# A planned state-space and feed-forward kernel: a new order of work, and dummy products in TensorE's planned pauses

## The chip, the cores and the metric

The kernel runs on one core of a Trainium2 chip. The metric is the device time of one execution in microseconds (us). A core has TensorE for matrix products (PE in the profile, its weight loads PEld), VectorE (DVE), ScalarE (ACT), GpSimd (POOL) and SyncE (SP), which issues the DMAs here. Each engine carries out its own list of instructions strictly in order; the engines wait for one another through semaphores.

## The reference

There are 4 batches, 8 heads, 768 positions, head size 32 and state size 16. A linear recurrence runs along the positions and its result goes through a feed-forward layer with 2048 hidden units. The recurrence is written by chunks:

```python
cum = np.cumsum(log(a) of the chunk)
L = np.exp(cum[i] - cum[j]) * (i >= j)
y_intra = ((Cc @ Bc.T) * L) @ xc
y_inter = (Cc @ state) * exp(cum)
state = exp(cum[-1]) * state + (Bc * exp(cum[-1] - cum)).T @ xc
# all y of the heads side by side: x of 3072 x 256
h = x @ w_in
out = (h - np.tanh(h)) @ w_out
```

## The kernel before, in words

**The recurrence.** Positions are cut into 28 chunks of up to 112 (7 for each batch); the 16 state rows are put in front of a chunk's 112 rows as if they were positions, so that a chunk is one product over 128 rows. The first three chunks (`first_tile`) get their decay matrix from sums on TensorE (`cp`) and exponentials on ScalarE with a bias `ncum`. The other 25 (`chunk_a`) get it from a product of two bf16 tables `lt_c` and `rt_c` (9 rows deep, PE L455) that are put together from the running sums: VectorE splits the sums in three bf16 parts (`split`), SyncE writes them to memory (`cum`, L767) and reads them back into the tables (L773 and L775, eight DMAs for the first 7 chunks and eight for the rest). Ahead of these DMAs, `lt_c` is filled with ones (ACT L712), and `rt_c` with the ones times a sign that alternates over the partitions (DVE L433, two operations for each of the two spans). For every chunk then follow the exponential (ACT L465), the multiplication with the `att` product (DVE L469), the causal mask (POOL L472), and `chunk_y`: the product `y` (PE L497), the new state copied into the next chunk's operand (ACT L510), and `y` split in a high and a low part (ACT L517, DVE L522). One `att` tile and one `y` tile exist, so chunk follows chunk.

**The feed-forward layer.** 12 tiles of 256 positions; 8 steps for each tile. A step is `mm1` (12 products into `ph`, L548), tanh, a subtraction, a split in high and low (`act`), and `mm2` (12 products into `o`, L598). The first four tiles are gone through in four sweeps of two steps, with partial sums kept in `pt` (`keep`), the others in one go; `store` adds up and sends the result out. Weights arrive as 64-bit floats (`raw`, 1 MB for each of the 8 steps) and are turned into a high and a low part `wh`, `wl` by `conv` (two operations on ACT, five on DVE).

**What sets the order.** All operations are recorded with an engine, a cost and their inputs and outputs in `Order`; a list scheduler (`schedule`) places them by priority against a model with one queue for each engine, `plan` improves the priorities by 16 rounds and 1500 random changes, and `issue` emits the instructions in the order of the planned starts. The costs are numbers in the calls `op(engine, cost, ...)`. Pools of tiles fix how many of each tile live at once: two `ph`, one `o`, one `att`, one `y`.

## Time and profile before

| | |
|---|---|
| median of 3 runs | 341.84 us (340.10 to 342.27) |
| profiled execution | 341.82 us |
| its span | 340.1 us |
| PE busy | 325.4 us (96%) |
| DVE, ACT, POOL busy | 227.0, 193.0, 58.1 us |
| PE busy in the first 60 us (six windows of 10) | 7.96, 6.78, 6.54, 9.97, 7.64, 10.00 us |
| mean granted TensorE clock | 0.968 of full speed |

The span runs from the first to the last instruction; the execution's time is 1.7 us longer. Busy time is the time in which at least one instruction of the engine runs. The granted clock is a share of TensorE's full speed. In a row of the trace, the first number is the start and the second the length in us, and square brackets hold the idle time of the engine before it with what ended it. In the table of windows, a row holds the stretch, its length, then busy us and the number of instructions of PE, PEld, DVE, ACT and POOL, the granted clock, the DMA share and GB/s.

### The profile page before, as it was taken

What the parts mean: (1) busy time and instruction counts of PE and PEld (TensorE: products, weight loads), DVE (VectorE), ACT (ScalarE), POOL (GpSimd) and SP (SyncE); (2) the same over time, 40 slices, a digit from 0 to 9 for tenths busy, and PEclk for the clock granted to TensorE, in tenths of its full rate; (3) what the DMA queues carried; (4) which work ended last, traced back from release to release, by engine and by line L of the source; (5) the groups of instructions that cost most, each with busy time, mean ns of one, the idle gap of its engine ahead of it and who ended that gap; (6) DMA issues with size and microseconds to landing.
All of it is one profiled execution on the core that took longest, in us unless ns stands there. A gap on an engine that the chain in (4) does not pass through costs nothing.

```text
span 340.1 us, 8905 instructions
## 1 busy us (share of the span) xinstructions
PE 325.4 (96%) x3772; PEld 313.0 (92%) x3772; DVE 227.0 (67%) x339; ACT 193.0 (57%) x403; POOL 58.1 (17%) x69
## 2 busy tenths in 40 slices
PE   7839979999999999999999999999999999999995
PEld 6738879999999999999999999999999999999995
DVE  4996797999899875645655555654745554654552
ACT  7855977787564453544655555545555545544451
POOL 1544354350000110100311210210301110110000
PEclk9955989999999999999999999999999999999999
DMA  7929657714000011101110200300200000000100
GB/s 161 308 59 322 171 144 196 225 44 143 1 2 3 0 62 46 48 2 46 60 47 19 76 2 2 91 2 9 87 2 1 33 2 2 33 0 2 33 0 32
DMA packets 12471, 21.39 MB, mean 63 GB/s; under 512 B 2848, under 2 KB 7648, under 8 KB 12432
## 3 DMA queue, kind: packets, MB, share of 16 engines
q1 hardware_dynamic: 12432, 20.84, 21.6%
q8 instruction: 29, 0.48, 0.6%
q14 instruction: 10, 0.08, 0.1%
HBM read 17.51 MB, written 3.32 MB: 61 GB/s over the span
## 4 chain that ended last, share of the span: by engine, by line
PE 85%; DVE 6%; DMA 4%; SPq 2%; issue 1%; ACT 1%
PE o L598 40%; PE ph L548 38%; PE y L497 3%; DMA raw<-w_d 3%; PE att L461 3%; DMA bc<-bc_d 1%; PE att L455 1%; SPq L773 1%; DVE lt L407 1%; DVE wm L313 1%; PE y L505 1%; DVE wv L310 1%; DVE wm L305 1%; DVE wl L324 1%; SPq L775 0%
## 5 line engine op out<-in xcount | busy, mean ns | idle before, releaser
L562 ACT ACTIVATE g<-ph 128x512 f32<-128x512 f32 x96 | 57.4, 598 | 87.2 <-PE ph L548 86.5
L566 DVE TENSOR_TENSOR g<-ph,g 128x512 f32<-128x512 f32 x96 | 65.9, 689 | 59.7 <-ACT g L562 59.7
L548 PE MATMUL ph<-xh,wh 128*128 128x256 f32 x384 | 100.4, 285 | 0.0
L548 PE MATMUL ph<-xh,wl 128*128 128x256 f32 x384 | 99.1, 282 | 0.0
L577 DVE TENSOR_TENSOR gl<-g,gh 128x512 fp32r<-128x512 f32 x96 | 66.9, 700 | 26.9 <-ACT gh L570 25.7
L548 PE MATMUL ph<-xl,wh 128*128 128x256 f32 x384 | 76.4, 281 | 0.0
L570 ACT CAST gh<-g 128x512 fp32r<-128x512 f32 x96 | 59.1, 618 | 28.8 <-DVE g L566 27.3
L548 PEld LDWEIGHTS ph<-xh,wh 128*128 128x128 f32 x384 | 73.9, 192 | 1.0 <-issue 0.4
L548 PEld LDWEIGHTS ph<-xh,wl 128*128 128x128 f32 x384 | 74.1, 193 | 0.0
L472 POOL TENSOR_SCALAR_AFFINE_SELECT lt<-lt 128x896 f32<-128x896 f32 (+1 forms) x25 | 34.0, 1360 | 202.1 <-DVE lt L469 202.1
L598 PE MATMUL o<-gh,wh 128*128 128x256 f32 x384 | 63.0, 286 | 0.0
L548 PEld LDWEIGHTS ph<-xl,wh 128*128 128x128 f32 x384 | 59.5, 193 | 0.0
L598 PE MATMUL o<-gh,wl 128*128 128x256 f32 x384 | 59.4, 277 | 0.0
L598 PE MATMUL o<-gl,wh 128*128 128x256 f32 x384 | 59.3, 277 | 0.0
L598 PEld LDWEIGHTS o<-gh,wh 128*128 128x128 f32 x384 | 50.9, 188 | 2.7 <-issue 0.2
L598 PEld LDWEIGHTS o<-gh,wl 128*128 128x128 f32 x384 | 51.0, 188 | 0.0
L598 PEld LDWEIGHTS o<-gl,wh 128*128 128x128 f32 x384 | 50.8, 188 | 0.0
L469 DVE TENSOR_TENSOR lt<-att,lt 128x896 f32<-128x896 f32 (+1 forms) x25 | 26.7, 1067 | 7.2 <-ACT lt L465 7.2
L465 ACT ACTIVATE lt<-att 128x896 f32<-128x896 f32 (+1 forms) x25 | 22.6, 903 | 6.5 <-PE att L461 4.7
L510 ACT COPY x<-y 16x64 f32<-16x64 f32 x96 | 19.6, 204 | 8.9 <-DVE xl L522 7.5
L497 PE MATMUL y<-lt,x 128*32 128x112 f32 (+1 forms) x448 | 17.4, 276 | 5.5 <-POOL bc L355 2.9
L497 PEld LDWEIGHTS y<-lt,x 128*32 128x32 f32 x448 | 10.4, 113 | 9.2 <-POOL bc L355 3.1
(70 smaller groups left out, 232.4 us busy)
## 6 DMA issues: line engine op xcount, KB each, us to landing
raw<-w_d SPq DMA_DIRECT2D x16, 512.0 KB
x<-x_d SPq DMA_DIRECT2D x14, 256.0 KB
bc<-bc_d SPq DMA_DIRECT2D x56, 60.0 KB
out_d<-ob SPq DMA_DIRECT2D x24, 128.0 KB
braw<-bn_d SPq DMA_DIRECT2D x14, 112.0 KB
cum<-parts SPq DMA_DIRECT2D x1, 168.0 KB
rt_c<-cum SPq DMA_DIRECT2D x4, 27.0 KB
lt_c<-cum SPq DMA_DIRECT2D x4, 27.0 KB
```

What stands on the lines that cost most here:

```text
L461: nc.tensor.matmul(out=at_[:, i, 2 + w, :], lhsT=bb[r, w], rhs=cc[r, w, 0:q], start=True, stop=True)
L465: nc.scalar.activation(k["l"][:, :, 0:q].rearrange("p (i w) q -> p i w q", i=4), k["a"][:, :, 0:2, :], AF.Exp)
L469: nc.vector.tensor_tensor(out=lt, in0=k["a"][:, :, 2:4, :], in1=lt, op=ALU.mult)
L472: nc.gpsimd.affine_select(out=k["l"][:, :, 0:q], in_=k["l"][:, :, 0:q], pattern=[[0, H], [1, q]], compare_op=ALU.is_ge, fill=0.0, base=N, ...
L497: nc.tensor.matmul(out=y[D * h : D * h + D, hg * Q : hg * Q + q], lhsT=d["x"][:, cg, P * hg + D * h : P * hg + D * h + D], rhs=k["l"][:, 4 ...
L510: nc.scalar.copy(grp[(ck + 1) // CPG]["x"][0:N, (ck + 1) % CPG, 2 * D * i : 2 * D * i + 2 * D], k["y"][D * i : D * i + N, H * D : H * D + ...
L548: nc.tensor.matmul(out=ph[:, j, :], lhsT=w_[:, u, 0, k, j * P : (j + 1) * P], rhs=d[("xh", "xl")[p]][:, k, ts], start=p == 0 and k == 0 an ...
L562: nc.scalar.activation(g, gs[t, u][0], AF.Tanh)
L566: nc.vector.tensor_tensor(out=g, in0=ph, in1=g, op=ALU.subtract)
L570: nc.scalar.copy(gh, gs[t, u][1])
L577: on.tensor_tensor(out=gl, in0=g, in1=gh.bitcast(F32), op=ALU.subtract)
L598: nc.tensor.matmul(out=po[t, seg][:, e, :], lhsT=w_[:, u, 1, j, e * P : (e + 1) * P], rhs=g[:, j, :], start=u == seg[0] and k == 0 and j = ...
```

## The change

- The search for the order: other costs for many operations, six starts of the random climb in place of one (seeds 5 to 10 in place of one seed), and a rule that the parts of one load are issued in turn.
- Dummy products: where the plan has a pause on TensorE of over 0.35 us in the first 65 us of planned time, `issue` now calls `fill`, which puts (pause - 0.35) / 0.215 products of ones with ones behind the operation, of the same form as those of `warm`. They write to a part of the tile `pq2` (one PSUM tile of the pool that `o` uses) that nobody reads. They start once `pq2` exists and end with the first `mm2`, which takes that tile's place.
- Work moves between engines: the filling of `lt_c` with ones from ACT to POOL; the identity rows of the three `braw` tiles (`stay`) from DVE to POOL; the sign product of `rt_c` for the second span (two operations of 2304 columns) from DVE to POOL, while that of the first span stays on DVE; the copy of the sums (`rows`) and their negation (`ncum`) from DVE to ACT.
- The partial sums `pt` and the outgoing tiles `ob` (four and two buffers) become one ring of six, which `rows` and `rest` use before; the first four tiles are added up in place.

The diff, cut to its core (further costs change as the two in the first lines of `conv` do):

```diff
+LULL, SPARE, PIECE = 65.0, 0.35, 0.215
+NPT = 6
-    ROUNDS, JITTER, SEED, CLIMB, RAMP = 16, 0.3, 133908, 1500, 110.0
+    ROUNDS, JITTER, SEED, CLIMB, RAMP, STARTS = 16, 0.3, 5, 1500, 110.0, 6
...
                 if dma and self.ops[j][0] == "DMA":
                     chain.add(j)
+                    soft.add(j - 1)
                     hard |= self.before[n]
...
     def plan(self):
+        _, span, start, _ = min((self.climb(random.Random(self.SEED + k)) for k in range(self.STARTS)), key=lambda b: b[0])
+        return span, start
...
         _, start = self.plan()
-        for i in sorted(range(n), key=lambda i: (start[i], i)):
+        order = sorted(range(n), key=lambda i: (start[i], i))
+        pe = [i for i in order if self.ops[i][0] == "PE"]
+        lull = {i: start[j] - start[i] - self.ops[i][1] for i, j in zip(pe, pe[1:])}
+        for i in order:
             if self.ops[i][2]:
                 self.ops[i][2]()
+            if start[i] < LULL and lull.get(i, 0.0) > SPARE:
+                self.fill(int((lull[i] - SPARE) / PIECE))
...
-            op("ACT", 1.0 * k, lambda s=s: fn0(s), r=n_r, w=[n_v[i]])
+            op("ACT", 1.17 * k, lambda s=s: fn0(s), r=n_r, w=[n_v[i]])
...
+    def fill(pieces):
+        one = nc.const_aps.tensor(1.0, (P, P), F32)
+        for _ in range(pieces if "pq2" in misc else 0):
+            nc.tensor.matmul(out=misc["pq2"][0:32, 3 * P :], lhsT=one[:, 0:32], rhs=one, start=True, stop=True)
...
-                    op("DVE", (0.3, 0.8)[s], lambda w=w, sl=sl: nc.vector.tensor_scalar(
+                    eng, on = (("DVE", nc.vector), ("POOL", nc.gpsimd))[s]
+                    op(eng, (0.45, 2.5)[s], lambda w=w, sl=sl, on=on: on.tensor_scalar(
                            out=rt_c[:, w, sl], in0=lt_c[:, sl], scalar1=par[:, w : w + 1], scalar2=None, op0=ALU.mult),
...
+            misc.pop("pq2", None)
             if u == seg[0]:
                 po[t, seg] = ps_o.tile([P, 2, TT], F32, tag="po", name=f"o{t}_{u}")
...
-        n_pt[t] = slot("pt", NSW)
+        n_pt[t] = slot("pt", NPT)
...
-        name = op.pieces(slot("ob", 2), 2)
+        name = [n_pt[t]] * 2 if t < NSW else op.pieces(slot("pt", NPT), 2)
...
         for t in braws:
-            nc.vector.tensor_copy(out=t[0:N].rearrange("p c (h n) -> p (c h) n", h=H),
+            nc.gpsimd.tensor_copy(out=t[0:N].rearrange("p c (h n) -> p (c h) n", h=H),
...
-        nc.scalar.copy(v, nc.const_aps.tensor(1.0, (P, 1), F32).broadcast_to(v.shape))
+        nc.gpsimd.memset(v, 1.0)
...
-            nc.vector.tensor_copy(out=rows[r], in_=misc["pr"][r, 0:2])
+            nc.scalar.copy(rows[r], misc["pr"][r, 0:2])
...
+    def negate():
+        nc.scalar.activation(ncum.rearrange("p h c -> p (h c)"), misc["pq"][:, 0:NHC], AF.Copy, scale=-1.0)
...
+    op.fill = fill
     op.issue()
```

How the change stands in the lists of the engines. TensorE before, around the second and third `y` of the first tile, down to the first product of the tables (a number behind a name tells buffers apart; `y` is the chunk's product, `att` of `rt_c` the first decay product, `ph` an `mm1`):

```order
L384 MATMUL cp_1_304<-upto,la 128x112 x4
L497 MATMUL y_323<-lt_239,x_151 32x112 x8
L505 MATMUL y_323<-x_151,bw_250 16x32 x8
L497 MATMUL y_369<-lt_289,x_159 32x112 x8
L505 MATMUL y_369<-x_159,bw_269 16x32 x8
L455 LDWEIGHTS lt_c
L455 MATMUL att_392<-rt_c,lt_c 128x224
```

The same place now; `pq` is the tile that takes the dummy products:

```order
L400 MATMUL cp_1_298<-upto,la 128x112 x4
L389 MATMUL pq_202<-const-float32-1.0 32x128 x4
L514 MATMUL y_329<-lt_228,x_146 32x112 x8
L522 MATMUL y_329<-x_146,bw_259 16x32 x8
L389 MATMUL pq_202<-const-float32-1.0 32x128 x13
L514 MATMUL y_384<-lt_272,x_233 32x112 x8
L522 MATMUL y_384<-x_233,bw_317 16x32 x8
L389 MATMUL pq_202<-const-float32-1.0 32x128 x6
L472 LDWEIGHTS lt_c
L472 MATMUL att_424<-rt_c,lt_c 128x224
```

23 dummy products stand here in three places, and four more stand behind the first `ph`; there are no others in the program.

VectorE before, from the multiplication of the first chunk on (`wm`, `wv`, `wl` belong to `conv`, `lt` is a chunk's decay matrix):

```order
L407 TENSOR_TENSOR lt_200<-att_190,lt_200 128x448 x2
L324 TENSOR_TENSOR wl<-wv_163,wh 128x512
L305 TENSOR_SCALAR wm_161<-raw_129 128x512
L407 TENSOR_TENSOR lt_239<-att_190,lt_239 128x448
L433 TENSOR_SCALAR rt_c<-lt_c,par 128x896
L310 TENSOR_SCALAR wv_163<-wv_163 128x512
L313 SCALAR_TENSOR_TENSOR wm_161<-wv_163,wm_161 128x512
L407 TENSOR_TENSOR lt_239<-att_190,lt_239 128x448
L317 SCALAR_TENSOR_TENSOR wv_163<-wv_163,wm_161 128x512
L522 TENSOR_TENSOR xl_318<-y_272,xh_309 128x2x112
L407 TENSOR_TENSOR lt_289<-att_190,lt_289 128x448
L433 TENSOR_SCALAR rt_c<-lt_c,par 128x896
```

The same place now:

```order
L423 TENSOR_TENSOR lt_187<-att_192,lt_187 128x448 x2
L321 TENSOR_SCALAR wv_171<-wv_171 128x512
L316 TENSOR_SCALAR wm_169<-raw_140 128x512
L328 SCALAR_TENSOR_TENSOR wv_171<-wv_171,wm_169 128x512
L450 TENSOR_SCALAR rt_c<-lt_c,par 128x896 x2
L423 TENSOR_TENSOR lt_228<-att_192,lt_228 128x448 x2
```

Both sign products of the first span (`rt_c`) now stand together ahead of the second chunk's multiplications; before, the first of these multiplications stood ahead of both, and six operations stood between the two.

GpSimd now, from its constants to the first mask of a later chunk (`bc` holds B and C of two chunks, `bw` their weighted B):

```order
L706 AFFINE_SELECT after<-after 128x128
L733 MEMSET lt_c 128x896
L733 MEMSET lt_c 128x2304
L728 COPY braw_99<-idn 16x256
...
L428 AFFINE_SELECT lt_272<-lt_272 128x448 x2
L450 TENSOR_SCALAR rt_c<-lt_c,par 128x2304 x2
L366 COPY bc_241<-idn 128x2x2x16
L489 AFFINE_SELECT lt_456<-lt_456 128x896
```

The two products of the second span stand behind the masks of the first tile and ahead of the operand `bc` of chunks 4 and 5 and of the first later mask; before, `bc` and one `bw` stood there alone.

More of the change, by code (lines that the diff above doesn't have):

```diff
@@ L355, in fn_c @@
             nc.gpsimd.tensor_copy(out=bb[:, :, :, 0:N], in_=idn.unsqueeze(1).unsqueeze(1).broadcast_to([P, 2, CPG, N]))
[L357 to L358 removed]
+        op("POOL", 0.38, fn_c, r=["idn"], w=[d["n_bc"]])
+        op("POOL", 0.95, fn_b, r=["wdec", "bi", d["n_b"]], w=[d["n_bw"]])
     def qlen(ck):
@@ L722, in tile_ssm_moe @@
     op("ACT", 1.4, lambda: table(0), w=["tab"])
-    op("POOL", 1.6, consts_pool, w=["upto", "after", "pid"])
-    op("DVE", 0.25, logs, r=["al"], w=["a"])
-    op("ACT", 0.4, lambda: nc.scalar.activation(la.rearrange("p h (b c) -> p c b h", b=NB), a_sb, AF.Ln), r=["a", "tab"], w=["la"])
-    op("DVE", 1.2, consts_dve, r=["pid"], w=["idn", "par"])
+    op("POOL", 1.3, consts_pool, w=["upto", "after", "pid"])
+    op("DVE", 0.28, logs, r=["al"], w=["a"])
+    op("ACT", 0.61, lambda: nc.scalar.activation(la.rearrange("p h (b c) -> p c b h", b=NB), a_sb, AF.Ln), r=["a", "tab"], w=["la"])
+    op("DVE", 0.9, consts_dve, r=["pid"], w=["idn", "par"])
     op("ACT", 1.4, lambda: table(1), r=["la"], w=["tab"])
-    op("DVE", 0.6, stay, r=["idn"], w=["bi"])
+    op("POOL", 1.2, stay, r=["idn"], w=["bi"])
     l_c = op.pieces("lt_c", 2)
     r_c = op.pieces("rt_c", 2)
-    op("ACT", 0.9, lambda: ones(0), w=[l_c[0]])
-    op("ACT", 2.2, lambda: ones(1), r=["tab"], w=[l_c[1]])
+    op("POOL", 0.9, lambda: ones(0), w=[l_c[0]])
+    op("POOL", 2.2, lambda: ones(1), w=[l_c[1]])
     for G in range(2):
@@ L777, in tile_ssm_moe @@
     n_pr = slot("y", 1)
-    op("PE", 0.8, sums_rows, r=["la", "upto"], w=[n_pr])
-    op("PE", 0.34, lambda: sums_cols(upto, "pq"), r=["la", "upto"], w=[n_pr])
-    op("DVE", 0.36, lambda: split(0), r=[n_pr], w=["rows"])
-    op("DVE", 0.33, lambda: nc.vector.tensor_scalar(out=ncum.rearrange("p h c -> p (h c)"), in0=misc["pq"][:, 0:NHC],
-                                                    scalar1=-1.0, scalar2=None, op0=ALU.mult), r=[n_pr], w=["ncum"])
-    op("DVE", 1.4, lambda: [split(i) for i in range(1, 6) if i != 4], r=["rows"], w=["parts"])
+    op("PE", 0.6, sums_rows, r=["la", "upto"], w=[n_pr])
+    op("PE", 0.5, lambda: sums_cols(upto, "pq"), r=["la", "upto"], w=[n_pr])
+    op("ACT", 0.42, lambda: split(0), r=[n_pr], w=[n_rows])
+    def negate():
+        nc.scalar.activation(ncum.rearrange("p h c -> p (h c)"), misc["pq"][:, 0:NHC], AF.Copy, scale=-1.0)
+    op("ACT", 0.38, negate, r=[n_pr], w=["ncum"])
+    op("DVE", 1.54, lambda: [split(i) for i in range(1, 6) if i != 4], r=[n_rows], w=[n_rest, "parts"])
     op("SP", 0.42, put_parts, r=["parts"], w=["cum3"], dma=KB)
     n_pq2 = slot("po", 1)
-    op("PE", 0.33, lambda: sums_cols(after, "pq2"), r=["la", "after"], w=[n_pq2])
-    op("ACT", 0.22, lambda: nc.scalar.activation(wdec.rearrange("p h c -> p (h c)"), misc["pq2"][:, 0:NHC], AF.Exp),
+    op("PE", 0.5, lambda: sums_cols(after, "pq2"), r=["la", "after"], w=[n_pq2])
+    op("ACT", 0.41, lambda: nc.scalar.activation(wdec.rearrange("p h c -> p (h c)"), misc["pq2"][:, 0:NHC], AF.Exp),
        r=[n_pq2], w=["wdec"])
```

67 lines of the change are left out of this document (34 added, 33 removed).

## The prediction

> **What bounds the kernel now.** I read the page first, then the busy time by windows, then TensorE's instructions in order of time up to 70 us, and last, for each pause found there, what the other engines and the DMA queue did.
>
> ```profile
> span 340.1 us, 8905 instructions
> PE 325.4 (96%) x3772; PEld 313.0 (92%) x3772; DVE 227.0 (67%) x339; ACT 193.0 (57%) x403; POOL 58.1 (17%) x69
> PEclk9955989999999999999999999999999999999999
> ```
>
> TensorE is the bound and is idle for 340.1 - 325.4 = 14.7 us. Each digit is the granted clock in 8.5 us, in tenths: it is lower only in the first six. The last row of the table below shows TensorE busy from 55 us to the end but for the last 3.5 us. So an edit is worth what it changes before about 55 us. The windows are cut where the clock changed (17.78, 34.85, 48.44, 51.85), distances that are multiples of 3.41 us. Columns: stretch, length, busy us of PE, PEld, DVE, ACT, POOL, then the granted clock, the DMA share and GB/s.
>
> ```profile
> 7.54:10.95 3.41, 2.65 (x42) 2.21 (x42) 3.24 (x8) 3.41 (x10) 0.29 (x1) 1.00 1.05 333
> 10.95:14.37 3.42, 2.82 (x50) 2.52 (x49) 3.42 (x7) 3.42 (x14) 3.04 (x5) 1.00 1.09 285
> 14.37:17.78 3.41, 2.02 (x51) 1.71 (x40) 3.38 (x7) 1.94 (x10) 1.92 (x3) 1.00 1.07 240
> 17.78:21.19 3.41, 0.99 (x32) 0.83 (x27) 3.18 (x7) 2.92 (x10) 1.48 (x3) 0.50 0.12 21
> 24.60:28.02 3.42, 3.37 (x30) 3.18 (x31) 1.85 (x4) 1.85 (x2) 0.00 (x0) 0.50 0.85 247
> 28.02:31.43 3.41, 3.41 (x31) 2.99 (x30) 3.04 (x5) 2.00 (x3) 1.90 (x1) 0.50 1.01 354
> 31.43:34.85 3.42, 3.42 (x59) 3.01 (x57) 1.93 (x3) 1.49 (x7) 1.56 (x2) 0.50 1.04 300
> 41.67:45.03 3.36, 2.80 (x49) 2.43 (x49) 3.36 (x5) 3.16 (x8) 1.80 (x1) 1.00 0.74 188
> 45.03:48.44 3.41, 1.62 (x57) 1.41 (x54) 3.41 (x6) 2.47 (x4) 2.14 (x2) 1.00 0.74 215
> 48.44:51.85 3.41, 3.41 (x17) 3.41 (x18) 2.54 (x3) 2.41 (x8) 1.93 (x2) 0.51 0.38 100
> 55.26:340.10 284.84, 281.29 (x3137) 273.68 (x3136) 182.42 (x264) 152.62 (x306) 34.82 (x35) 1.00 0.12 36
> ```
>
> Where TensorE was busy for 2.02 of 3.41 us (59%), or 1.62 (48%), the clock fell to half at the window's end; at 2.65 (78%) and more it stayed. It came back only after three full windows (24.60 to 34.85), or after one (48.44 to 51.85). The pauses behind these windows:
>
> ```profile
> 0.84 3.49 PE L719 MATMUL warm<-const-float32-1.0 128*32 128x128 f32 x16 [0.84 <-PEq L873]
> 17.64 0.92 PE L497 MATMUL y<-lt,x 128*32 128x112 f32 x16 [1.39 <-POOL lt L412]
> 21.70 0.97 PE L497 MATMUL y<-lt,x 128*32 128x112 f32 x16 [2.93 <-POOL bc L355]
> 24.65 0.37 PE L455 MATMUL att<-rt_c,lt_c 9*128 9x224 bf16 x4 [1.76 <-DMA lt_c<-cum]
> 25.81 0.58 PE L548 MATMUL ph<-xh,wh 128*128 128x256 f32 x1
> 28.67 0.37 PE L455 MATMUL att<-rt_c,lt_c 9*128 9x224 bf16 x4
> 33.81 0.37 PE L455 MATMUL att<-rt_c,lt_c 9*128 9x224 bf16 x4
> 47.69 0.59 PE L497 MATMUL y<-lt,x 128*32 128x112 f32 x16 [1.15 <-DVE g L566]
> 80.05 1.36 PE ph L548 x12
> PE att L455 <- DVE lt L469: 1.2, 2, 0.6
> ```
>
> The last two rows are from other views. One is from the chain that ended last: a group of 12 feed-forward products takes 1.36 us at full clock, where the first group in the program took 28.67 - 25.81 = 2.86 at half. The other is from the table of waits: `att` waited twice for a multiplication on VectorE, 1.2 us in all.
>
> **Term 1: an earlier first table product.** At 24.65 TensorE waits for `lt_c` from the DMAs. Behind them, in the chain, stand SyncE and a sign product on VectorE:
>
> ```profile
> 17.83 0.38 DVE rt_c L433
> 18.26 0.84 SPq L773
> ...
> 22.41 0.71 SPq L773
> L773 SPq EVENT_SEMAPHORE  x1: 1814/1814/1814, 16.4 to 16.4; - x1
> 9.58 0.37 SPq L767 DMA_DIRECT2D cum<-parts  x1
> ```
>
> SyncE's last wait ran from 16.4 to 18.2 us and ended with VectorE's second sign product; what it had waited for until 16.4 I take to be the landing of `cum`, issued at 9.58. In the changed list both sign products stand ahead of the second chunk's multiplications, so they should be done by about 14, and the landing becomes the last event. Before `cum`, the queue now holds one `x` and one `braw` load less; I let it land at 16.0. The eight issues (18.26 to 22.41 + 0.71) take 4.9 us and the last transfer landed 24.65 - 23.12 = 1.5 us later, which gives 22.4. The third `y` must also be past (21.70 + 0.9 before; its masks come about 1 us earlier now), and six dummy products follow it. I take 22.65 for the first `att`: **-2.0 us**; bounds 0 (the masks set the time and the dummies fill it up) and -3.
>
> **The dummy products.** `warm` has the same form: 16 rows for 8 products in 3.49 us, 0.436 each. Their end falls on the grid of the clock (17.78 - 4 x 3.41 = 4.14), so I take them as run at half and estimate 0.218 at full. The 4, 13 and 6 dummies then take 0.87, 2.83 and 1.31 us, in the places of the pauses 1.39, 2.93 and 1.76: covered. The four behind the first `ph` (0.87) stand in a wait that the next term shows. If a pause shrinks, its dummies delay the real work by what is missing, up to their sum, 27 x 0.218 = 5.9 us. With them, 14.37 to 24.60 is nearly full, against 59% and less.
>
> **Term 2: no half clock from 17.78 to 34.85.** In the three windows from 24.60, 3.37 + 3.41 + 3.42 = 10.2 us of busy TensorE at half clock would shrink by the ratios of the rows (`y` 0.97 to 0.59, a `ph` group 2.86 to 1.36) to about 5.6: a gain of 4.6 if TensorE alone set the pace. The serial chain of a chunk sets another limit, as there is one `att` tile:
>
> ```profile
> 26.02 0.92 ACT L465 ACTIVATE lt<-att 128x896 f32<-128x896 f32 x1 [1.98 <-PE att L461]
> 26.97 1.09 DVE L469 TENSOR_TENSOR lt<-att,lt 128x896 f32<-128x896 f32 x1 [1.57 <-ACT lt L465]
> ```
>
> Exponential 0.92, multiplication 1.09, some 0.9 for the `att` products at full clock and 0.4 for hand-overs make 3.3 us for a chunk. The two periods from 24.65 to 33.81 took 9.16 and would take 6.6. I take the chain's **-2.5**; bounds 0 and -4.6.
>
> [...]
>
> **Term 3: 38 to 52 us.** Here TensorE waits for VectorE (1.2 + 1.15 = 2.35 us), which is busy throughout (3.36 of 3.36, 3.41 of 3.41), and then loses 3.41 x 0.45 = 1.5 us to the second half clock. No dummies stand here, since the tile has gone to `mm2`. VectorE's list becomes shorter and its inputs come earlier:
>
> ```profile
> L433 DVE TENSOR_SCALAR rt_c<-lt_c,par 128x2304 bf16<-128x2304 bf16 x2 | 1.6, 808 | 0.0
> ```
>
> It sheds these two, 1.6 us, here, and it had 3.42 - 1.85 = 1.6 us idle between 24.60 and 28.02 alone, part of which an earlier chunk can use. I take the clock's 1.5 and half of the waits: **-2.5**; bounds 0 and -3.9. What is late next is again VectorE, with the conversions between the chunks.
>
> **Term 4: the sign products on POOL.** POOL's speed at them is not in the trace.
>
> ```profile
> L472 POOL TENSOR_SCALAR_AFFINE_SELECT lt<-lt 128x896 f32<-128x896 f32 x21 | 28.4, 1353 | 177.2 <-DVE lt L469 177.2
> L348 POOL TENSOR_TENSOR bw<-braw,wdec 128x256 f32<-128x256 f32 x14 | 13.6, 976 | 28.7 <-PE y L505 28.7
> 20.38 0.58 POOL L412 TENSOR_SCALAR_AFFINE_SELECT lt<-lt 128x448 f32<-128x448 f32 x1 [1.75 <-DVE lt L407]
> 28.13 1.90 POOL L472 TENSOR_SCALAR_AFFINE_SELECT lt<-lt 128x896 f32<-128x896 f32 x1 [4.85 <-DVE lt L469]
> 38.59 1.70 POOL L348 TENSOR_TENSOR bw<-braw,wdec 128x256 f32<-128x256 f32 x2
> 38.72 1.06 DVE L310 TENSOR_SCALAR wv<-wv 128x1024 f32<-128x1024 f32 x1
> 20.84 0.69 DVE L310 TENSOR_SCALAR wv<-wv 128x1024 f32<-128x1024 f32 x1
> ```
>
> Bounds for one product of 2304 columns: VectorE's own 0.8, and 976 ns / 256 x 2304 = 8.8 us by POOL's two-input product. The mask, with one input like this one, gives 1353 / 896 x 2304 = 3.5, the nearest row; two take 7.0. The cover is POOL's quiet time between its last small mask (20.38) and first large one (28.13). From about 19.7 they run to 26.7, and `bc` of the fifth chunk and the next mask, wanted at about 26, wait: +1. VectorE's L310 took 1.06 in place of 0.69 beside POOL at work; two or three such for the longer operations add another +1. Together **+2.0**; bounds 0 and +5.
>
> [...]
>
> **Edits at nothing.** The ones of `lt_c` leave ACT, where the larger fill stood ahead of the first exponential; what that brings is in term 1's earlier masks. On POOL these ones and `stay` lie before the first `bc` copy:
>
> ```profile
> 7.96 0.29 POOL L355 COPY bc<-idn 128x64 f32<-128x64 f32 x1 [5.81 <-DMA bc<-bc_d]
> ```
>
> The 5.81 us of waiting hide them; if they take longer, the first `att` slips by the excess. `rows` and `ncum` go to an ACT that has room. The ring of six and the store in place lie beyond 100 us, where TensorE is always busy (281.29 of 284.84, the rest being the end); without that cover a store would add its 0.7. The order beyond 55 us has the same groups of products, hence no gain.
>
> **Sum.** -2.0 - 2.5 - 2.5 + 2.0 = -5.0 against the profiled 341.8 us (340.1 of span and 1.7 around it), which equals the median of 341.84. Forecast: **336.8 us**. [...]
>
> **Rivals.** A change of under 1% (338.4 to 345.3) is about what a measurement of this kernel cannot tell from none.
>
> A, slower: the dummies themselves run at half clock. For: they exist only from `pq2` to the first `mm2`, and the windows ahead (78% and 82%) are not far above the 59% that closed the clock. If the clock falls at 10.95, 23 dummies take 10.0 us where 1.39 + 2.93 + 1.76 = 6.1 were idle (+3.9), and products of 2.82 + 2.02 us slow down ahead of them, of which pauses take up about half (+2). The gain of term 1 is gone, the half clock stays up to the first chunks: 347 us, less if the dummies reopen it early. It decides below some 70% busy in 7.54 to 10.95. Against: the dummies of the third place alone keep later windows full. 8%.
>
> B, no change: POOL and VectorE stand still for each other, as L310 did, but for the whole of a product, which makes 5 us of each. Then POOL is free at about 30, the chunk chain moves back by 3, and terms 2 and 3 halve: -2.0 - 1.3 - 1.2 + 3 = -1.5, 340.3 us. 24%. At 8.8 us each it would be free at 37, nine later than 28.13, against gains of 7: about 344 to 346. 4%.
>
> C, better: POOL hides and TensorE sets the pace: -3 - 4.6 - 2 = -9.6 at most, say 333. 9%.
>
> D, the dummies don't hold the clock, but cost nothing, since what counts is something else than busy time (24.60 to 31.43 was full without a raise). Then terms 1 and half of 3 remain against term 4: 340.5 us. 5%. Against: `warm`, of the same form, preceded a full clock.
>
> **Chances and range.** The forecast has 50%, from 334 to 338.4. Faster by over 1%: forecast, C and a part of B, 50 + 9 + 6 = 65%. Within 1%: the rest of B, D, the milder half of the slow POOL case, 18 + 5 + 2 = 25%. Slower: 8 + 2 = 10%. The range takes in B and D and most of C, and leaves A and the very best out: 332.5 to 343.0.
>
> **What would show it.** Clock 1.00 from 4.14 to at least 40 us and dummies of about 0.22 us: term 2 right; 0.43: A. The first `att` at 22 to 23: term 1. SyncE waiting for `cum` and not for `rt_c`: its reason. POOL's two products at 3 to 4 us each, and the first large mask by 28: term 4; VectorE rows of over 2 us beside them: B. No half-clock window near 48: term 3. The prediction is wrong if the first `att` is not before 24, or if TensorE pauses for more than 3 us in all between 35 and 55.

## The result: 3% slower, and the profile after

The changed kernel takes 351.82 us (median of 4 runs, 350.77 to 352.19) against 341.58 us for the kernel before (4 runs, 340.10 to 342.27): a ratio of 1.030 with a 95% interval of 1.026 to 1.034. The forecast was 336.8 us, faster. A ratio here compares executions of the two kernels from the same run and leaves out those over 1.5% above the fastest of their kernel, so it can differ a little from the quotient of the medians. The profiled execution took 351.62 us. From its page:

```profile
span 349.9 us, 8995 instructions
PE 330.6 (94%) x3826; PEld 317.2 (91%) x3826; DVE 238.5 (68%) x332; ACT 192.7 (55%) x403; POOL 73.9 (21%) x76
PEclk9995699989999999999999999999999999999999
```

TensorE is idle for 349.9 - 330.6 = 19.3 us, where it was 14.7; VectorE is busy for 11.5 us more and GpSimd for 15.8 more. The clock is still low in the fourth and fifth slices, and a little in the ninth. The windows of after, cut where its clock changed, show where (columns as in the prediction: stretch, length, busy us of PE, PEld, DVE, ACT, POOL, granted clock, DMA share, GB/s):

```profile
13.64:17.05 3.41, 3.41 (x67) 2.99 (x65) 2.76 (x5) 3.35 (x15) 1.84 (x4) 1.00 0.94 268
17.05:20.46 3.41, 2.73 (x53) 2.51 (x51) 3.41 (x7) 2.83 (x8) 2.19 (x3) 1.00 0.11 25
23.87:27.29 3.42, 0.80 (x12) 0.53 (x4) 3.42 (x1) 0.00 (x0) 3.42 (x1) 1.00 1.02 357
30.70:34.11 3.41, 2.05 (x9) 1.34 (x9) 3.41 (x1) 0.00 (x0) 3.41 (x1) 0.50 0.27 92
34.11:37.53 3.42, 1.40 (x21) 1.20 (x20) 3.31 (x3) 1.54 (x2) 2.44 (x4) 0.50 0.24 61
```

Up to 23.87 the dummy products do what the forecast wanted: the stretch that closed the clock before stays at 1.00. Then, from 23.87 on, TensorE has little to do for 14 us. VectorE and GpSimd are shown busy all the time, but with one instruction each for a whole window ("x1"). GpSimd and VectorE there, in order of time:

```profile
20.79 13.66 POOL L450 TENSOR_SCALAR rt_c<-lt_c,par 128x2304 bf16<-128x2304 bf16 x2
34.40 0.77 POOL L366 COPY bc<-idn 128x64 f32<-128x64 f32 x1
36.15 0.99 POOL L489 TENSOR_SCALAR_AFFINE_SELECT lt<-lt 128x896 f32<-128x896 f32 x1 [0.98 <-DVE lt L486]
```

```profile
3.67 1.39 DVE L710 TENSOR_SCALAR a_sb<-a_sb 128x224 f32<-128x224 f32 x1 [1.48 <-DMA a_sb<-a_d]
...
21.27 0.68 DVE L321 TENSOR_SCALAR wv<-wv 128x1024 f32<-128x1024 f32 x1
21.98 6.49 DVE L324 SCALAR_TENSOR_TENSOR wm<-wv,wm 128x1024 uint32<-128x1024 uint32 x1
28.40 0.38 DVE L539 TENSOR_TENSOR xl<-y,xh 128x224 fp32r<-128x224 f32 x1
28.70 6.38 DVE L328 SCALAR_TENSOR_TENSOR wv<-wv,wm 128x1024 uint32<-128x1024 uint32 x1
35.00 1.08 DVE L486 TENSOR_TENSOR lt<-att,lt 128x896 f32<-128x896 f32 x1
```

The two sign products take 6.8 us each on GpSimd, not 3.5. Beside each of them one operation of VectorE with two inputs stands still until about its end: 6.49 and 6.38 us, where the same two operations took 1.23 and 1.54 in the kernel before:

```profile
21.57 1.23 DVE L313 SCALAR_TENSOR_TENSOR wm<-wv,wm 128x1024 uint32<-128x1024 uint32 x1
22.82 1.54 DVE L317 SCALAR_TENSOR_TENSOR wv<-wv,wm 128x1024 uint32<-128x1024 uint32 x1
```

What waits behind on the two engines is the low part of `y` (`xl`), the multiplication of the first `att`, `bc` of chunks 4 and 5, and the first large mask, which came at 28.13 before and comes at 36.15 now. TensorE, and what it and SyncE waited for:

```profile
21.85 1.50 PE L389 MATMUL pq<-const-float32-1.0 128*32 128x128 f32 x12
23.28 0.28 PE L472 MATMUL att<-rt_c,lt_c 9*128 9x224 bf16 x4
...
28.83 0.79 PE L565 MATMUL ph<-xl,wh 128*128 128x256 f32 x2 [4.16 <-DVE xl L539]
...
30.83 1.92 PE L389 MATMUL pq<-const-float32-1.0 128*32 128x128 f32 x8
36.13 0.37 PE L472 MATMUL att<-rt_c,lt_c 9*128 9x224 bf16 x4 [3.38 <-DVE lt L486]
```

```profile
PE att L472 <- DVE lt L486: 5.6, 4, 3.4
PE ph L565 <- DVE xl L539: 4.2, 1, 4.2
...
SPq L794 <- POOL bc L366: 4.9, 1, 4.9
```

The second table product comes at 36.13; before it was 28.67. That is 7.5 us, most of the 9.8 by which the span grew, and the four dummies behind the first `ph` run at half clock (1.92 for 8 rows). SyncE, too, stood for 4.9 us. The view names `bc`, but the load (L794, the first of `lt_c` for the second span) went at 34.47, while `bc` ran from 34.40 to 35.17. What had just ended, at 34.45, was the second sign product, which reads the part of `lt_c` that this load overwrites.

### The profile page after: what moved, and what is told of

The parts are those of the page before. It is cut to its first block, busy times and chain, and to the rows that moved or that the text cites. A ratio compares the mean times of both kernels' runs of the same rounds, so it can differ in the third digit from the quotient of the medians.

```text
span 349.9 us, 8995 instructions
## 1 busy us (share of the span) xinstructions
PE 330.6 (94%) x3826; PEld 317.2 (91%) x3826; DVE 238.5 (68%) x332; ACT 192.7 (55%) x403; POOL 73.9 (21%) x76
## 3 DMA queue, kind: packets, MB, share of 16 engines
q1 hardware_dynamic: 12432, 20.84, 21.3%
## 4 chain that ended last, share of the span: by engine, by line
PE 82%; DVE 12%; issue 3%; DMA 1%; ACT 1%; SPq 0%; POOL 0%; POOLq 0%; DVEq 0%
PE o L616 38%; PE ph L565 37%; PE y L514 3%; DVE wv L328 3%; PE att L478 2%; DVE wl L335 2%; DMA raw<-w_d 1%; DVE lt L486 1%; DVE gl L594 1%; PE att L472 1%; DVE lt L423 1%; DVE wm L316 1%; DVE g L583 1%; DVE xl L539 1%; PE y L522 1%
## 5 line engine op out<-in xcount | busy, mean ns | idle before, releaser
L594 DVE TENSOR_TENSOR gl<-g,gh 128x512 fp32r<-128x512 f32 x96 | 68.5, 717 | 23.1 <-ACT gh L587 21.2
L489 POOL TENSOR_SCALAR_AFFINE_SELECT lt<-lt 128x896 f32<-128x896 f32 (+1 forms) x25 | 31.6, 1263 | 205.8 <-DVE lt L486 204.1
L514 PE MATMUL y<-lt,x 128*32 128x112 f32 (+1 forms) x448 | 16.6, 265 | 2.2 <-DVE xl L539 1.9
L359 POOL TENSOR_TENSOR bw<-braw,wdec 128x256 f32<-128x256 f32 x14 | 12.3, 880 | 21.2 <-PE y L522 21.1
```

The lines of the kernel that those rows point to most:

```text
L359: nc.gpsimd.tensor_tensor(out=d["b"].rearrange("p c (h n) -> p c h n", h=H), in0=d["braw"].rearrange("p c (h n) -> p c h n", h=H), in1=wd. ...
L489: nc.gpsimd.affine_select(out=k["l"][:, :, 0:q], in_=k["l"][:, :, 0:q], pattern=[[0, H], [1, q]], compare_op=ALU.is_ge, fill=0.0, base=N, ...
L514: nc.tensor.matmul(out=y[D * h : D * h + D, hg * Q : hg * Q + q], lhsT=d["x"][:, cg, P * hg + D * h : P * hg + D * h + D], rhs=k["l"][:, 4 ...
L594: on.tensor_tensor(out=gl, in0=g, in1=gh.bitcast(F32), op=ALU.subtract)
```

## The experiments

The theory after the result: the whole loss comes from the two sign products on GpSimd, by way of VectorE, which stands still beside them, or of GpSimd's own queue and what waits for its end, and the rest of the change would have brought a part of the forecast's gain. The rivals: the dummies cost, the fills of `lt_c` on GpSimd cost, or the new order is worse in itself.

### The sign products back on VectorE

The list stays word for word as it is; only the engine of two instructions changes.

```diff
-                    eng, on = (("DVE", nc.vector), ("POOL", nc.gpsimd))[s]
+                    eng, on = (("DVE", nc.vector), ("POOL", nc.vector))[s]
```

> Edit: the two sign products of the second span are issued on VectorE, at the same place of the same plan; everything else is the changed kernel. Theory P (the shared read path): in the changed kernel each product (6.83 us on GpSimd) held up one scalar_tensor_tensor of the conversion on VectorE for its whole length (6.49 and 6.38 us in place of about 1.2). Without them these two should take 1.2 to 1.3 us, the first y after them should not wait, and the time should fall by 10.5 us of stall less 1.6 us for the products on VectorE, and by some 2 us more where the clock then stays up: 338 to 342 us. Rival O (the new order itself is worse): the two operations become short, but the time stays above 346.

A "read path" that the two engines share was my supposition, here and in the runs with pieces; the runs show which operation took how long beside which, and not a path.

Measured: 339.68 us, a ratio to the kernel before of 0.9965 (0.9932 to 0.9999). Its page, VectorE and TensorE in order of time, and TensorE's waits:

```profile
span 337.2 us, 8996 instructions
PEclk9999999999999999999999999999999999999999
```

```profile
22.87 1.23 DVE L324 SCALAR_TENSOR_TENSOR wm<-wv,wm 128x1024 uint32<-128x1024 uint32 x1
24.02 0.81 DVE L450 TENSOR_SCALAR rt_c<-lt_c,par 128x2304 bf16<-128x2304 bf16 x1
25.04 1.22 DVE L328 SCALAR_TENSOR_TENSOR wv<-wv,wm 128x1024 uint32<-128x1024 uint32 x1
```

```profile
23.44 0.28 PE L472 MATMUL att<-rt_c,lt_c 9*128 9x224 bf16 x4
27.49 0.28 PE L472 MATMUL att<-rt_c,lt_c 9*128 9x224 bf16 x4
31.04 0.28 PE L472 MATMUL att<-rt_c,lt_c 9*128 9x224 bf16 x4 [0.21 <-DVE lt L486]
```

```profile
PE att L472 <- DVE lt L486: 2.3, 4, 1.4
PE y L514 <- DVE xl L539: 1.9, 2, 1.2
```

The whole loss is gone: 351.82 - 339.68 = 12.1 us for two instructions (11.5 by the ratios). VectorE pays 0.81 for a product and its neighbours take 1.23 and 1.22. What is left is the gain of everything else in the change: 0.35%, 1.2 to 1.8 us, not the 7 that the first three terms of the forecast add up to. No other kernel here had a lower ratio, though several lie within its interval.

### GpSimd writes, but doesn't read

A fill of the same place in the place of each product (so this kernel leaves out the second span's signs):

```diff
-                    op(eng, (0.45, 2.5)[s], lambda w=w, sl=sl, on=on: on.tensor_scalar(
+                    op(eng, (0.45, 2.5)[s], lambda w=w, sl=sl, on=on: on.memset(rt_c[:, w, sl], 1.0) if on is nc.gpsimd else on.tensor_scalar(
```

> Edit: the two sign products of the second span stay on GpSimd at the same place but are replaced by fills with ones of the same size (left out: the signs of the second span, so the sums of the later chunks are wrong). GpSimd then only writes SBUF and reads nothing. Theory P: the scalar_tensor_tensor operations beside them take 1.2 to 1.6 us, and the time is 337 to 342 us. Rival Q (any long GpSimd operation holds VectorE up): they take as long as the fill beside them, about 2.0 us or more each (the two fills of lt_c took 2.84 us for 3200 columns together).

Measured: 340.82 us, ratio 0.9975 (0.9941 to 1.0010). GpSimd, then VectorE:

```profile
22.05 5.06 POOL L450 MEMSET rt_c<- 128x2304 bf16 x2
```

```profile
22.57 2.58 DVE L321 TENSOR_SCALAR wv<-wv 128x1024 f32<-128x1024 f32 x1
25.18 1.23 DVE L324 SCALAR_TENSOR_TENSOR wm<-wv,wm 128x1024 uint32<-128x1024 uint32 x1
```

The two-input operation isn't held by a fill (1.23), but a one-input one is (2.58, against 0.68). With the products it was the other way round: L321 took 0.68 and L324 stood still. So what GpSimd does decides which operation of VectorE is held, and the two-input operations of after are held by the product and not by just any long operation of GpSimd. A product and a fill differ in the reading, but not in that alone (5.06 us for two against 13.66).

### The products in nine pieces

If VectorE's standing still is what costs, pieces of 256 columns should cure it, since an operation would then wait for one piece at most.

```diff
+                    op(eng, (0.45, 2.5)[s], lambda w=w, sl=sl, on=on, step=(7, 2)[s]: [on.tensor_scalar(
+                           out=rt_c[:, w, c0 : c0 + step], in0=lt_c[:, c0 : c0 + step], scalar1=par[:, w : w + 1], scalar2=None, op0=ALU.mult)
+                           for c0 in range(sl.start, sl.stop, step)],
```

> Edit: the changed kernel with each sign product of the second span on GpSimd cut in 9 pieces of 256 columns, at the same place. Theory P (the read path is held for one instruction at a time): VectorE gets in between two pieces, no operation of the conversion takes more than 2.5 us, and the time falls to 339 to 344. Rival S (the two engines share the path by bandwidth, or GpSimd's queue keeps it): the two operations of the conversion still take 5 us or more together with it, and the time stays above 348. The pieces also give GpSimd's own speed: those with no two-input operation beside them give its price alone.

Measured: 355.46 us, ratio 1.041 (1.036 to 1.047): worse than the change itself, and far from the 339 to 344 expected. GpSimd, VectorE, and TensorE's longest wait:

```profile
21.66 19.42 POOL L450 TENSOR_SCALAR rt_c<-lt_c,par 128x256 bf16<-128x256 bf16 x18
```

```profile
22.86 1.30 DVE L324 SCALAR_TENSOR_TENSOR wm<-wv,wm 128x1024 uint32<-128x1024 uint32 x1
```

```profile
PE att L479 <- POOL bc L366: 13.7, 1, 13.7
```

VectorE runs undisturbed (1.30), and still the kernel loses 16 us against the list with the products on VectorE: the copy `bc` waits behind GpSimd's 19.4 us, and TensorE waits 13.7 for `bc`. SyncE's load of `lt_c`, too, went only at 41.11, when the last piece had ended. So a long stay on GpSimd is a second cause that suffices by itself. The median piece took 0.92 us and the longest 1.88; the eighteen took 19.42, where 18 x 0.916 make 16.5. The shortest whole product here took 6.10 us (in the old list, below); from that and 916 ns for a piece I estimate 2.53 ns for a column and 0.27 us for an instruction.

The same pieces, told to the planner at 0.92 us each and planned anew:

> Edit: the changed kernel with each second-span sign product on GpSimd as 9 operations of 256 columns, each told to the plan at 0.92 us, its price measured in e8, and the plan searched again. Theory L (the loss comes from GpSimd's own length, which the plan took for 2.5 us each, and from what stands behind it): told the price, the plan puts operands and masks between the pieces, and the loss shrinks to 342 to 347 us. Rival X (GpSimd is the wrong place whatever the plan knows): still above 349.

356.01 us, ratio 1.038 (1.032 to 1.044), against 342 to 347 expected. The planner put five pieces ahead of `bc` and eleven behind it, so that masks waited behind those. Its price did not hold there: in the profiled execution (359.39 us) the five took 9.59 us in place of 5 x 0.92 = 4.6, beside VectorE's conversions, and the eleven 13.25 in place of 10.1; the last two, at 46.57 beside an idle VectorE (8.42 us up to 48.80), took 1.82. So GpSimd's pieces, too, take longer beside VectorE at work. A plan that knew this was not tried.

### The two causes one at a time

In after both end at the same time, at about 35 us, so the profile of after can't divide the loss between them. The first run has GpSimd's queue without the standing still of the two-input operations: fills in place of the products, repeated until they last about as long. It leaves out the second span's signs.

```diff
+                    op(eng, (0.45, 2.5)[s], lambda w=w, sl=sl, on=on: [on.memset(rt_c[:, w, slice(sl.start, sl.start + m)], 1.0) for m in ((18, 18, 18), (18, 18, 6))[w]] if on is nc.gpsimd else on.tensor_scalar(
```

> The changed kernel with its list as it is, but GpSimd fills the second span's part of rt_c with ones, again and again, for about as long as its two sign products took: five fills of 2304 columns (2.53 us each in the run with single fills) and one of 768, 13.5 us in all against the products' 13.66. It leaves out the second span's signs. The fills don't hold VectorE's two-input operations (1.23 and 1.22 us beside them in the run with single fills, against 6.49 and 6.38 beside the products), so what is left of the loss is what stands behind on GpSimd's queue (bc of chunks 4 and 5, the mask) and on SyncE's. Queue theory: nearly the whole loss is there, since bc again comes at about 34.5 us and the second att at about 35.5 (36.13 in the changed kernel): 349 to 351.5 us. Stall theory: VectorE's lost 11 us are what cost, and with its list ahead of time GpSimd's wait costs only the pause it makes: 343 to 346 us. In between, 346 to 349: both are needed.

Measured: 348.50 us, ratio 1.020 (1.012 to 1.027). GpSimd, VectorE, TensorE:

```profile
20.78 12.39 POOL L450 MEMSET rt_c<- 128x2304 bf16 x6
33.11 0.24 POOL L366 COPY bc<-idn 128x64 f32<-128x64 f32 x1
```

```profile
23.91 1.23 DVE L324 SCALAR_TENSOR_TENSOR wm<-wv,wm 128x1024 uint32<-128x1024 uint32 x1
```

```profile
33.41 1.21 PE L478 MATMUL att<-bc 16*128 16x112 f32 x16 [5.33 <-POOL bc L366]
```

Two things differ from the queue in after: VectorE's L321 was held here too (2.58 us, as beside the single fills, where the kernel took 340.82), and SyncE did not wait, since a fill doesn't read `lt_c`: its load went at 28.97.

The second run has the standing still nearly without the queue: one product goes back to VectorE, so that GpSimd is done before its next work is due.

```diff
-                    eng, on = (("DVE", nc.vector), ("POOL", nc.gpsimd))[s]
+                    eng, on = (("DVE", nc.vector), ("POOL", (nc.vector, nc.gpsimd)[w]))[s]
```

> The changed kernel with one of the two sign products of the second span back on VectorE, the other on GpSimd at the same place. GpSimd should be busy with it for 6.8 us, from about 21 to 28, and one two-input operation of VectorE (L324) should stand still until it ends; bc of chunks 4 and 5 then comes at about 28, 1.5 us after the place where the second att stood ready in the list without any (27.49). If the loss grows with GpSimd's time: half of 12.1, so 345.7 us. If only that counts which passes the wait GpSimd had anyway (5.91 us before its first mask in the list without any): 341 to 344 us.

Measured: 352.10 us (349.42 to 354.52), ratio 1.029 (1.019 to 1.039), and not to be read for this question: in the profiled execution, one of the 354.5, TensorE's products took about twice as long until 24 us (3.60 us for the first 16 rows of `cp`, where the run with fills had 1.84 for 15), and the first `att` came at 31.01 (of its other executions there is no trace). The kernel was run once more with a longer warm-up (11 products in place of 8):

> One sign product of the second span on GpSimd and one on VectorE, as before, with 11 products in place of 8 in the opening warm-up. In the profiled execution of the run without them the products after the warm-up took twice as long until 24 us (the first cp group 3.60 us for 16 rows, where the run with fills on GpSimd had 1.84 for 15), so the first att came 7.7 us late for a reason that has nothing to do with GpSimd; a longer warm-up should leave such executions out. GpSimd then has its one product from about 21 to 28 us. In proportion to GpSimd's time: 345.7 us. Loss only past the 5.91 us that GpSimd waited anyway: 341 to 344. If already the first product costs most of the loss, as the two quicker executions of that run (349.4 and 349.8) would have it: 348 to 350.

Measured: 347.02 us, ratio 1.015 (1.009 to 1.022). GpSimd, VectorE, TensorE:

```profile
20.91 6.54 POOL L450 TENSOR_SCALAR rt_c<-lt_c,par 128x2304 bf16<-128x2304 bf16 x1
27.40 0.75 POOL L366 COPY bc<-idn 128x64 f32<-128x64 f32 x1
32.64 1.94 POOL L489 TENSOR_SCALAR_AFFINE_SELECT lt<-lt 128x896 f32<-128x896 f32 x1 [4.49 <-DVE lt L486]
```

```profile
21.39 6.67 DVE L450 TENSOR_SCALAR rt_c<-lt_c,par 128x2304 bf16<-128x2304 bf16 x1
```

```profile
30.31 0.80 PE L565 MATMUL ph<-xl,wh 128*128 128x256 f32 x2 [5.52 <-DVE xl L539]
```

GpSimd has time to spare here (it waits 4.49 us for VectorE's multiplication), and none of the six longest waits of TensorE ends on its work or on a DMA (the longest is the one for `xl`, the shortest 0.3 us). So this loss is VectorE's standing still; it hit VectorE's own sign product, 6.67 in place of 0.81, which has one input beside its scalar. (The longer warm-up alone was run only with another set of dummies, below, and changed nothing clear of noise there.) By the ratios, against the 0.9965 without any product on GpSimd: the queue costs 2.3% (7.9 us of 341.5) for 12.4 us of GpSimd's time, one standing still of 5.9 us 1.9% (6.4 us), and the change with both 3.4% (11.5 us). The intervals leave each of the first two uncertain by about 2.5 us either way, so that they overlap in after is likely but not shown. The expectation "only past the wait that GpSimd had" is refuted. The run with fills fell into the band that I had put down for "both are needed"; that reading doesn't hold either, since each of the two runs has only one of the causes and loses several us.

### The same move in the old list

```diff
-                    op("DVE", (0.3, 0.8)[s], lambda w=w, sl=sl: nc.vector.tensor_scalar(
+                    op("DVE", (0.3, 0.8)[s], lambda w=w, sl=sl, on=(nc.vector, nc.gpsimd)[s]: on.tensor_scalar(
```

> Edit: the kernel before with nothing changed but the engine of the two sign products of the second span, which go to GpSimd at their places in the old list. Theory P: each product takes 5 to 7 us there, an operation of VectorE with two inputs in SBUF that falls beside one (wl, wm or gl) takes 4 us or more in place of 0.7 to 1.2, and the time is 347 to 353 us: the move alone carries the loss. Rival O' (the products hurt only at their place in the new list): below 344 us.

Measured: 346.60 us, ratio 1.017 (1.011 to 1.023), just below the 347 to 353 expected. GpSimd's two products, and the two-input operation of VectorE beside each:

```profile
23.57 7.08 POOL L433 TENSOR_SCALAR rt_c<-lt_c,par 128x2304 bf16<-128x2304 bf16 x1
32.10 6.10 POOL L433 TENSOR_SCALAR rt_c<-lt_c,par 128x2304 bf16<-128x2304 bf16 x1
```

```profile
28.17 3.10 DVE L324 TENSOR_TENSOR wl<-wv,wh 128x1024 fp32r<-128x1024 f32 x1
32.79 5.50 DVE L577 TENSOR_TENSOR gl<-g,gh 128x512 fp32r<-128x512 f32 x1
```

`wl` took 1.22 and `gl` 0.68 in the kernel before. So the loss isn't one of the new order. It is half as large here, where the two products stand apart with a mask between them; that this is the reason was not tried.

### The dummy products

Without any in the new list (signs on VectorE), and with them in the list of before:

```diff
-    op.fill = fill
+    op.fill = lambda pieces: None
```

> Edit: as e1, but without the 27 dummy products. Theory C (the dummies hold the clock): without them a window between 14 and 25 us is under 60% busy, the clock is at half when the first feed-forward products run, and the time is 2.5 to 5 us above e1. Rival D (the dummies don't matter): within 1 us of e1. Rival A' (the dummies only delay real work): 1 us or more below e1.

> Edit: the kernel before with its own list of work and only the dummy products added by the same rule; the old plan gives 13 of them ahead of the third y and 5 between the first table products and the first ph. Theory C (the clock is worth something by itself): the clock is back at full before 28 us, and the time falls by 1 to 3 us, to 338.5 to 341. Rival A (the clock has fallen before them, as nothing fills the pause ahead of the second y): the 13 dummies take 5.7 us in a pause of 2.9, the first ph comes 2 to 3 us later, and the time is 341 to 344. Rival D: no change within 0.5 us although the clock stays up.

Measured: 341.51 us, ratio 1.0007 (0.9973 to 1.0040), for the new list without dummies, against 0.9965 with them; 340.65 us, ratio 0.9984 (0.9955 to 1.0013), for the old list with 18 of them. So the new list without the dummies can't be told from the old one, and the dummies are worth about 0.4% in it, at the edge of what the runs can tell and less than the 2.5 to 5 us expected. In the old list no gain can be told from none.

Which of them count? The last six run into the first `att` (their row ends at 23.35, `att` starts at 23.28), so they might be what delays it. Two runs, each with the first ones alone, the new list's 4 and 13, and the old list's 13:

```diff
-            if start[i] < LULL and lull.get(i, 0.0) > SPARE:
+            if start[i] < LULL and lull.get(i, 0.0) > SPARE and len(self.made_fills) < 2:
```

> Edit: as e1 (second-span signs on VectorE, same list), with only the first two groups of dummy products, 4 and 13; the 6 ahead of the first table product and the 4 behind the first ph are left out. In e1 the 6 ran until the first table product started at 23.44, while its last DMA had been issued by 20.8 and the third y ended at 22.0. Theory W (dummies delay real work where the real pause is shorter than the planned one): the first table product starts at 22.2 to 22.8, and the time is 0.7 to 1.5 us below e1. Rival C2 (they are needed for the clock): the clock falls once more and the time is e1's or more.

> Edit: the kernel before with its own list and only the 13 dummies ahead of the third y; the 5 ahead of the first ph, which took 2.0 us there in e6 without a pause to fill, are left out. Over the 50 executions of the kernel before, its time rises by 0.25 to 0.29 us with each us at half clock. Theory W: about as much half clock as in e6 (7 to 10 us), the first ph earlier by 1 to 2 us, and 338.5 to 340 us. Rival: the two groups only replace each other, 340.3 to 341.5.

Measured: 342.04 us, ratio 1.0014 (0.9989 to 1.0039), and 341.15 us, ratio 0.9973 (0.9940 to 1.0006). TensorE in the first:

```profile
21.97 0.27 PE L474 MATMUL att<-rt_c,lt_c 9*128 9x224 bf16 x4
...
25.05 0.59 PE L567 MATMUL ph<-xl,wh 128*128 128x256 f32 x2 [1.68 <-DVE xl L541]
25.43 0.42 PE L567 MATMUL ph<-xh,wh 128*128 128x256 f32 x1
```

`att` does come 1.5 us earlier (21.97 against 23.44), as was expected, but three us later the products take 0.42 in place of 0.28, as they do at half clock (0.41 in after at 39.50, in a window whose clock was 0.50). Nothing is won; the kernel is slower than the one with all dummies, where 0.7 to 1.5 us less were expected. So the last six do delay the first `att`. Without any dummies it came at 22.78:

```profile
22.78 0.37 PE L472 MATMUL att<-rt_c,lt_c 9*128 9x224 bf16 x4
```

The dummies buy the clock with the time that they take; the last section puts a number to it. A longer warm-up in the same kernel:

> Edit: as e9, with 11 instead of 8 products in the warm-up, which fill the 1.4 us that TensorE waits for the first sums (later by 1.57 us than before, since the clamp waits for GpSimd's fills). In three of ten executions of e1 the clock opened a window late (3.4 to 4.8 us at half), and these took 341.2 in place of 338.7 to 339.9. Theory: no late opening, median 0.3 to 0.8 us below e9. Rival: no change within 0.3 us.

341.48 us, ratio 0.9986 (0.9961 to 1.0012): not to be told from the run without. That the clock opened late in three executions of the list with all dummies was my reading of their mean clocks (0.993 to 0.995); there is no trace of them.

### The ones on VectorE

GpSimd's fills of `lt_c` ran beside VectorE's clamp L710, which took 1.39 us in after and 0.28 before; it also began 0.45 later (3.67 against 3.22). So the first sums started at 5.85 in place of 4.28. Moved to VectorE (signs there too):

```diff
-        nc.gpsimd.memset(v, 1.0)
+        nc.vector.memset(v, 1.0)
```

> Edit: as e1, and the two fills of lt_c with ones also go from GpSimd to VectorE. In the changed kernel the clamp of a_sb on VectorE took 1.39 us beside GpSimd's fills, against 0.28 before, and the logarithm started 1.56 us later than before. Theory P2 (the fills delay the whole chain of running sums): the clamp takes about 0.3 us, the first product of the sums starts at about 4.4 in place of 5.85, and the time is 1.0 to 1.5 us below e1. Rival: the chain is then held by the landing of the first raw weights (7.14 in the changed kernel), and the time is within 0.5 us of e1.

> Edit: the changed kernel with all four sign products and the fills of lt_c on VectorE, and the plan searched again with these engines (costs 0.45, 0.8, 0.4 and 0.8 us), so that the list is made for it; dummies as in the changed kernel. If the plan's knowledge of the engine is worth something: 1 to 3 us below e1, 336.5 to 338.5. Rival (the lists differ only within what a measurement can tell): 338.7 to 341.

Measured: 340.52 us, ratio 0.9982 (0.9937 to 1.0026), and, with the order searched anew for it, 341.24 us, ratio 1.0007 (0.9973 to 1.0041). The expected gain did not come: the large fill took 1.98 us on VectorE and stood ahead of the clamp there, so the clamp began at 5.33 and the sums at 6.33. A place for the fill that costs nothing was not found.

## Why the prediction was wrong

**The failed step is term 4**, the sign products on GpSimd. It was put at +2.0 us with bounds 0 and +5; it measured +12.1 (351.82 against 339.68). Three things in it were wrong:

- *The price of a product.* I took 3.5 us from the mask's row, since that has one input like the product; it is 6.1 to 7.1, between the mask's 3.5 and the 8.8 scaled from the two-input row. The choice "nearest row" went by the number of inputs; a row of the same operation and type was not in the trace. The middle of the bounds 0.8 and 8.8, 4.8, would have been nearer, but too low as well.
- *VectorE.* I read from L310 (1.06 in place of 0.69 beside GpSimd) that the two disturb each other by a fraction, and added 1 us. One operation of VectorE stands still beside a product until about its end: 6.49, 6.38, 5.50, 6.67 us. I also misread the L310 row: at 38.72 it stood beside `bw` (38.59, two operations in 1.70 us, too short to show a hold of several us) and not beside a mask, and the 0.69 at 20.84 that I set against it was not free of GpSimd either. The fills didn't do that to the same operation: it took 6.49 beside a product and 1.23 beside a fill. Rival B had the standing still, without a difference between a product and a fill, and I gave it 28%.
- *The cover.* I let GpSimd start at 19.7 and be done by 26.7, in the quiet time up to 28.13. It started at 20.79 and was done at 34.45. What stood behind it I had named (`bc` of chunks 4 and 5, the mask); missing was SyncE, which waited 4.9 us for the products' end with the table loads for the second span and the loads behind them.

Rival B is what happened, but its prices came too low (5 us a product for 340.3 us, a value that no run shows, where the runs had 6.1 to 7.1; 8.8 for 344 to 346), because I counted only the shift of GpSimd's end and let terms 2 and 3 halve. A product costs more than its shift: VectorE's lost time is a second chain to TensorE (`xl`, 4.2 us of waiting), and TensorE loses the clock again (0.56 and then 0.50, behind a window in which it was busy for 0.80 of 3.42 us), so term 2 vanishes with it. By the points written down: the clock was 1.00 up to 27 us and not to 40; `att` came at 23.28, just outside 22 to 23; the products took 6.8 and not 3 to 4; VectorE had rows of over 2 us, the sign of B; the first large mask came at 36.15 and not by 28. TensorE idled for 20.00 - 16.09 = 3.9 us between 35 and 55, over the 3 us that I had named, 1.1 of it the end of the pause before the second `att`.

**Term 1** was right, and the dummies took a part of it back. SyncE no longer waits for the sign products; its loads begin at 14.50. Without any dummies the first `att` comes at 22.78, -1.9 us; with the first 17 alone at 21.97, -2.7; with all of them at 23.44, -1.2 and not -2.0 (all three without the GpSimd products). What set it was the third `y`, right behind which it stands in the first two, and not the loads: the last of the eight was issued at 19.68 in the third, against 22.41 in the kernel before. So what is missing is the last six dummies, which run in front of `att` when it is ready: they fill the time up, as bound 0 had it. GpSimd's fills, which I had put among the edits at nothing under GpSimd's own 5.81 us of waiting, do hold VectorE's clamp for 1.1 us, in these runs too (1.41 us with all dummies and 1.44 without any, for 0.28); that this cost the first `att` anything isn't shown.

**The dummy products** ran as forecast: 13 in 2.83 us, 0.218 each, at full clock. Rival A, the clock falling in the first windows, did not happen (1.00 up to 27.29).

**Term 2** was right in kind. With the signs on VectorE the half clock is gone (mean granted clock 0.998, against 0.968), and the two periods from the first `att` to the third take 31.04 - 23.44 = 7.6 us, where they took 9.16 and I had 6.6: -1.6 and not -2.5.

**Term 3** (-2.5) brought nothing. The second half clock is gone, but the waits for VectorE didn't shrink by half; they grew, `att` from 1.2 to 2.3 us, and `y` from 1.15 (for `g`) to 1.9 (for `xl`). The span without the GpSimd products fell by 340.1 - 337.2 = 2.9 us, and terms 1 and 2 as measured (1.2 + 1.6) use up 2.8 of them. VectorE's list seems to be the limit: it was busy for 19.93 of the 20.00 us from 35 to 55. The 1.6 us that I let it shed "here" were misplaced, as the two products stood at 24.59 and 30.01 in the kernel before, ahead of this stage; and in this run VectorE does them again. Where GpSimd filled in their place, VectorE was rid of them, and the time was no lower (340.82).

The first three terms together so gave 2.9 us in the profiled executions, of which that of the new list was 0.8 below its median, and 1.2 to 1.8 by ratio and medians, against 7.0. Of the 4.1 us that are missing in the profiled executions, 2.4 are term 3.

## What to carry to other kernels

An idle engine isn't free room: before work is moved to GpSimd, look up what VectorE runs beside it, since here each of the whole sign products held one VectorE operation, by 2 to 6 us, and look up what stands behind it on GpSimd's queue and what on SyncE's waits for its end. Price a moved operation by a run of it on its new engine; a row of another operation on that engine was off by a factor of two. A clock gained by dummy products is worth the difference between what it saves and what the dummies themselves delay, here 0.4% in the best of the runs.

## What the runs showed of the hardware

- **GpSimd and VectorE.** Beside GpSimd's products, held were operations with two inputs (6.49, 6.38, 5.50, 3.10) and also two with one input: VectorE's bf16 sign product (6.67 for 0.81) and, in the run with one product, L316 on raw words (6.39 for 0.77). Not held was L321, in float32, with 0.68. Beside GpSimd's fills it was L321 that was held (2.58 for 0.68), and the clamp (1.39 for 0.28). Beside pieces no operation of VectorE took more than 1.41 us (1.30 in the first of the two runs with pieces). It goes both ways: a product took 6.10 and 6.11 us where VectorE, at its start, was at an operation on a result of TensorE (`lt<-att`, `xl<-y`), and 6.54 to 7.08 where VectorE was at a conversion; five pieces took 9.59 beside VectorE's conversions, and two took 1.82 beside an idle VectorE. So L321 may have passed while the product itself still waited; that was not tried.
- **GpSimd's prices.** The bf16 product: 6.10 us at the least for 2304 columns and 0.916 for 256, by which I estimate 0.27 us and 2.53 ns for a column of 128 partitions. The fill of 2304 bf16 columns: 5.06 us for two; VectorE needed 1.98 for one and 0.81 for a product of that size.
- **What half clock costs, and what dummies cost.** The kernel before ran 93 times beside these experiments. From the granted clock of each execution its time at half clock, taken as 0.50 as in the windows above, is 2 x (1 - clock) x span: 10 to 24 us, median 17. Execution times follow it as 337.4 us + 0.27 us for each us at half clock (correlation 0.79). Terms 2 and 3 together were 5.0 us for the 22 us of the execution that I worked from, 0.23 for each: not too much by this line. But the kernels with dummies lie above it. The list with the signs on VectorE had 1.4 us at half clock in the median, for which the line gives 337.8, and took 339.68; with the first 17 dummies alone it had 10.6 us, for 340.2, and took 342.04; the old list with 18 had 6.8 us, for 339.2, and took 340.65. Without dummies the new list had 14.3 us, for 341.2, and took 341.51. So the dummies seem to give back 1.4 to 1.9 us of what the clock brings. This is an estimate; for the first and the third the line is drawn beyond the 10 to 24 us that it comes from.
- **A slow start that the clock's view doesn't show.** In the execution of 354.5 us with one product, the products behind the eight of the warm-up were slow: the first `cp` products took 3.60 us for 16 rows where another run had 1.84 for 15, until 24 us, while the view of the granted clock showed 1.00 all that time. So the view doesn't show every slow stretch, and the times at half clock above leave such a one out. The warm-up took 3.59 us there, as in the list with the signs on VectorE; why the products behind it were slow isn't shown. That execution was 5 us, 1.4%, above the quicker two of its kernel.
